# Both heads' choices in one copy, and three exponentials instead of four in the first halves

## The chip, the core and the metric

The kernel runs on one core of a Trainium2 chip. The metric is the device time of one launch in microseconds. The core has five engines that run side by side and wait for each other through semaphores: TensorE (PE in the profile; its weight loads, PEld, are shown apart), VectorE (DVE), ScalarE (ACT), GpSimd (POOL) and SyncE (SP). POOL and SP issue nearly all transfers here, POOL those that also convert float32 to bfloat16. Each engine works through its own instructions in the order in which they are written.

## What is computed

An attention with chunk selection, followed by a feed-forward network with a squared ReLU. There are 4 batches, 8 heads, 768 positions and 64 columns per head. Keys stand in 24 chunks of 32; each query keeps the 6 chunks with the highest upper bound.

```python
k_min = np.min(k_chunks, axis=3)
k_max = np.max(k_chunks, axis=3)
ub = np.sum(np.maximum(q[:, :, :, None, :] * k_min[:, :, None, :, :],
                       q[:, :, :, None, :] * k_max[:, :, None, :, :]), axis=-1)
ub = np.where(causal, ub, -1000000000.0)
top_chunks = np.argsort(ub, axis=-1)[..., -top_k:]
scores = scale * np.matmul(q, k.transpose(0, 1, 3, 2))
...
mask = sel & (pos[:, None] >= pos[None, :])
scores = np.where(mask, scores, -1000000000.0)
...
attn = attn / (np.sum(attn, axis=-1, keepdims=True) + 1e-09)
return np.matmul(attn, v).astype(np.float32)
...
h = np.maximum(x @ w_in, 0.0)
return (h * h @ w_out).astype(np.float32)
```

x has 3072 rows (tokens) and 512 columns (8 heads by 64); w_in is 512 x 2048, w_out 2048 x 512.

## The kernel before

**Slots.** A half is 384 queries of one batch (three tiles of 128). The eight halves run in the order of line 29: batches 0 and 1, first half; batches 0 and 1, second half; then batch 2 and batch 3, each first half and second half. Each half has four slots, one for each pair of heads, so slots 0 to 31 (`slots`, line 219). Slots 0 to 3, 4 to 7, 16 to 19 and 24 to 27 are first halves, 16 slots in all. A first-half query sees three key tiles at most, a second-half query six.

**Steps of a slot.** `step_T` transposes k and q on TensorE (`step_P` calls it in later slots). `extrema` takes minimum and maximum of each key chunk on DVE (L228, L232) and lays them out in `kbds` (L233). `relus_T` makes the positive and negative parts of q on ACT (L288). `place` copies k and q to `kqs` (L293). `step_U` makes the upper bounds `ub` on TensorE (L371 to L382), finds the sixth largest with MAX8 on DVE (L389) and writes with a comparison (L391) which chunks are out: in slots 0 to 3 next to q in `qn0`, in slots 4 to 11 in `chosen`. `step_V` transposes these flags on TensorE into a PSUM tile `qt` and copies them on DVE to rows 64 to 95 of `kqs` (L424 and L428 for slots 0 to 3, L434 and L439 for 4 to 11). From slot 12 on a transfer (`step_W`) does this. A score product therefore has 96 rows, 64 of the head and 32 of flags against a coded one-hot of the key's chunk, and the product itself masks the chunks.

**Scores.** `step_E(s, hh, n)` fills bank n of head hh with score products into a PSUM tile `ps` (L452), takes the exponential on ACT into the SBUF tile `e` (L458) and, for n = 1, lets POOL clear the upper triangle of the three diagonal blocks (`affine_select`, L462). `BANKS` says which key tile and which query tiles go to which columns: a first half has two banks per head, one of 512 columns and one of 256 (at columns 256 to 511); a second half has four. `col_of` finds a block's column again.

**Values.** `step_F(s, hh)` multiplies the blocks of `e` with v, which has a column of ones, into `po` (L478); after the second head DVE takes the reciprocal of the sums (L487) and multiplies (L488) into `x`. From slot 4 on a transposing transfer on SP brings x to `xT` (L492); for slots 0 to 3 `x_T` transposes on TensorE (L516) and `x_copy` copies on DVE (L522).

**Feed-forward.** When a half is done, `push` queues 16 up products (`ffn_up`: four matmuls into `ph`, L560, ReLU on ACT, L564, square on DVE, L566) and 12 down pieces (`ffn_down`: four matmuls each into `py`, L576, copy to `ob`, L582 or L584, and out). `f1()` takes one from the queue between the attention's steps. The first half pushes only up products; its down pieces come with the second `push`. The pieces of one output tile use the rows of w_out in order, the first two of them rows 0 to 1023, the other two the rest.

**PSUM.** `psS` has three banks (score tiles `ps`), `psF` two (`ph`), `psY` one (`py`), `psA` two (tag `att`, line 66). From `psA` come, each time the older of the two: `ub`, `qt`, `po` and the tile of `busy`. A new tile may be written when the last reader of the older one is done.

**Fillers.** `busy(n)` issues n matmuls of the identity into a tile nobody reads (L651).

**Order.** The order is written out by hand. Slots 0 to 3 run in the loop of lines 685 to 718: `step_E(s,0,0)`, k transposes and minimum of slot s+2, `step_E(s,0,1)`, `step_E(s,1,0)`, `busy(8)`, `step_U(s+1)`, `place` of k of slot s+1, `step_E(s,1,1)`, from slot 1 on `step_F(s-1, ...)`, `step_V(s+1)`, then q transposes, `relus_T` and the rest of `extrema` of slot s+2. In slot 3, `x_T` and `x_copy` of the first two pairs stand there, with `busy(10)`. Slots 4 to 31 run in the loop of lines 725 to 856; slot 4 starts with `step_E(4,0,0)`, `step_F(3, ...)`, k and q of slot 5, and `x_T` and `x_copy` of the other two pairs, one by one with `busy(8)` between, then `push(0)`.

**Transfers on POOL.** Loads are queued per slot with `at(slot, ...)` and issued by `go`: codes for batch 1, and w_in in two halves of 1024 columns, in slot 0; three v loads of batch 1 in slot 1; k and q of the third half in slot 2; w_out's first half in slot 3; codes and w_out's second half in slot 4. POOL's selections stand in the same queue.

Of the kernel before, what the change touches and what calls it, by code (L numbers as in the profile page):

```python
# [39 lines left out]
def kernel(  # L40
# [171 lines left out]
    def col_of(half, j, i):  # L212
        for n, bank in enumerate(BANKS[half]):
            for (at, jj, i0, m) in bank:
                if jj == j and i0 <= i < i0 + m:
                    return 512 * n + at + 128 * (i - i0)
        raise KeyError
# [199 lines left out]
    def step_V(s):  # L417
# [14 lines left out]
        qt = psA.tile([128, HB], BF16, tag="att", name="qt")  # L432
        for j in range(j0, HT):
            nc.tensor.matmul(  # L434
                qt[0:2 * CR, 128 * j:128 * (j + 1)],
                lhsT=chosen[s % 2][:, j].rearrange("r h c -> r (h c)"),
                rhs=ident, is_transpose=True, start=True, stop=True)
        for h in range(2):
            nc.vector.tensor_copy(  # L439
                kqs[b % 2][D:KR, p, 2 * half + 1, h, c:], qt[CR * h:CR * h + CR, c:])  # L440

    def step_E(s, hh, n):
        b, half, p = slots[s]
        t = st[s]
        if n == 0:
            t["e"][hh] = work.tile([128, 1920], BF16, tag="e", bufs=4, name="e")
# [21 lines left out]
    def step_F(s, hh):  # L468
# [5 lines left out]
        for i in range(HT):  # L474
            iq = HT * half + i
            for j in range(iq + 1):
                c = col_of(half, j, iq)
                nc.tensor.matmul(  # L478
                    po[:, hh, i, :], lhsT=t["e"][hh][:, c:c + 128],
                    rhs=vn[b % 2][:, 2 * p + hh, j, :],  # L480
                    start=(j == 0), stop=(j == iq))
# [128 lines left out]
    for g in range(2):  # L610
        at(0, load_w_in, 1024 * g, 1024 * g + 1024)
    for j in range(HT):
        at(1, load_vt, 1, j)
    for n in "kq":
# [70 lines left out]
    for s in range(NP):  # L685
# [9 lines left out]
        busy(8)  # L695
        step_U(s + 1)
        if not last:
# [8 lines left out]
        if last:  # L706
            x_T(0, 0, F)
        step_V(s + 1)
        if last:
            x_copy(0, 0, 0, 2, nc.vector.tensor_copy)  # L710
            busy(10)
        else:
            step_T(s + 2, F, Y, "q")
# [11 lines left out]
    for s, (b, half, p) in enumerate(slots):  # L725
# [16 lines left out]
        if s == NP:  # L742
            for n in range(hf):
                step_E(s, 0, n)
            step_F(s - 1, 0)
            step_F(s - 1, 1)
            step_P(s + 1)
            relus_T(s + 1)
            x_T(0, 1, F, (0,))
            x_copy(0, 1, 0, 1, nc.vector.tensor_copy)  # L750
            busy(8, *A)
            x_T(0, 1, F, (1,))
            x_copy(0, 1, 1, 2, nc.vector.tensor_copy)
# [143 lines left out]
```

## Time and profile before

| what | us |
|---|---|
| median of three runs | 268.06 (267.74 to 268.2) |
| the profiled execution, its own time | 268.22 |
| its span, first to last instruction | 266.5 |
| TensorE busy, of the span | 255.0 |
| ScalarE busy | 177.6 |
| VectorE busy | 162.4 |
| GpSimd busy | 92.3 |
| granted TensorE clock, mean | 1.000 |

How to read it: the page gives the busy time of each engine, and matmuls overlap in TensorE's pipe, so the duration of one (219 ns for a filler) is longer than the time from one start to the next. In rows of the timeline stand the start, the time covered, the engine, the line, the operation, output and inputs with their shapes, the count, and in brackets how long the engine had been idle and what ended that. The chain of waits follows the last instruction back: at each step to what released it, or to the instruction before it on its engine; a row has start, length and what it was. Groups have count, then busy time and mean duration in ns, then idle time before them. Stages from here on: the opening is slots 0 to 3, to about 25 us, when the first up product starts; then slots 4 to 7, to about 48 us, when the first down piece starts.

### The profile page before, as it was taken

To read this page: it belongs to the slowest core of one execution; us is meant where nothing else is said; L and a number is where in the kernel's file an instruction comes from. 1 tells how busy PE (TensorE), PEld (TensorE's weight loads), DVE (VectorE), ACT (ScalarE), POOL (GpSimd) and SP (SyncE) were. 2 spreads that over 40 slices of the span, in tenths; PEclk is the share of its full clock that TensorE was granted. 3 is DMA by queue.
4 is the path that set the end of the run, shared out by engine and by line. 5 is a ranking of instruction groups with operands and counts; after the bars stand their busy time and mean duration, and the time that the engine had idled before them with its cause. 6 is when DMAs were issued, how large, how long until landed. Compare 5 with 4: busy or idle time off the path is not lost.

```text
span 266.5 us, 6623 instructions
## 1 busy us (share of the span) xinstructions
PE 255.0 (96%) x2432; PEld 157.8 (59%) x2432; DVE 162.4 (61%) x618; ACT 177.6 (67%) x398; POOL 92.3 (35%) x138
## 2 busy tenths in 40 slices
PE   7789899999999999999999999999999999999995
PEld 7567555556666566655665566745565666645543
DVE  6788999666996468546875576555863233424411
ACT  5898879588976688845575777934685788614500
POOL 8996356426821425235611544320120111000000
PEclk9999999999999999999999999999999999999999
DMA  7999999999997799999995999995532220111022
GB/s 139 163 182 210 170 212 193 134 144 142 147 167 117 140 145 184 131 174 152 190 137 123 131 167 121 222 123 124 127 95 66 71 44 18 57 41 39 2 79 79
DMA packets 116817, 33.98 MB, mean 128 GB/s; under 512 B 103728, under 2 KB 112720, under 8 KB 116784
## 3 DMA queue, kind: packets, MB, share of 16 engines
q0 software_dynamic: 64640, 13.83, 65.5%
q1 hardware_dynamic: 51200, 19.33, 39.6%
q8 instruction: 19, 0.31, 0.5%
q10 hardware_dynamic: 944, 0.39, 0.5%
q14 instruction: 14, 0.11, 0.2%
HBM read 27.26 MB, written 6.29 MB: 126 GB/s over the span
## 4 chain that ended last, share of the span: by engine, by line
PE 79%; DMA 10%; DVE 6%; ACT 3%; issue 1%; SPq 0%; ACTq 0%; DVEq 0%; POOLq 0%
PE py L576 29%; PE ph L560 26%; PE ps L452 12%; DMA w_out<-in_moe_w_out_dram 7%; PE po L478 7%; DMA stage<-in_q_dram 2%; PE ub L375 2%; DVE km L336 2%; PE py L548 1%; ACT e L458 1%; PE idle L651 1%; PE tk L267 1%; DVE x L488 1%; DVE m L389 1%; DVE kq L428 1%
## 5 line engine op out<-in xcount | busy, mean ns | idle before, releaser
L458 ACT ACTIVATE e<-ps 128x512 bf16<-128x512 f32 x192 | 96.3, 551 | 17.6 <-PE ps L452 17.0
L560 PE MATMUL ph<-xT,w_in 128*128 128x384 bf16 x512 | 98.9, 326 | 0.2 <-ACT ht L564 0.2
L576 PE MATMUL py<-w_out,h 128*128 128x512 bf16 x368 | 88.1, 379 | 0.3
L564 ACT ACTIVATE ht<-ph 128x384 bf16<-128x384 f32 x128 | 62.5, 501 | 30.0 <-PE ph L560 29.6
L566 DVE TENSOR_TENSOR h<-ht 128x384 bf16<-128x384 bf16 x128 | 46.6, 374 | 57.4 <-ACT ht L564 56.9
L462 POOL TENSOR_SCALAR_AFFINE_SELECT e<-e 128x384 bf16<-128x384 bf16 x64 | 33.8, 535 | 127.1 <-ACT e L458 126.0
L560 PEld LDWEIGHTS <-w_in 128*128 128x128 bf16 x512 | 47.6, 97 | 30.7 <-issue 1.2
L452 PE MATMUL ps<-kq 96*128 96x384 bf16 (+2 forms) x320 | 57.4, 278 | 2.0 <-DVE kq L428 1.5
L576 PEld LDWEIGHTS <-h 128*128 128x128 bf16 x368 | 34.8, 97 | 35.7 <-issue 1.0
L452 PEld LDWEIGHTS <-kq 96*128 96x128 bf16 x320 | 26.4, 97 | 16.6 <-issue 2.1
L478 PEld LDWEIGHTS <-e 128*128 128x128 bf16 x672 | 25.4, 98 | 4.8 <-issue 0.8
L478 PE MATMUL po<-vn,e 128*128 128x65 bf16 x672 | 26.7, 194 | 0.7 <-DMA vn<-in_v_dram 0.7
L389 DVE MAX8 m<-ub 128x8 f32<-128x16 f32 (+4 forms) x160 | 16.2, 168 | 17.8 <-PE ub L382 10.7
L582 ACT COPY ob<-py 128x512 f32<-128x512 f32 x18 | 10.5, 585 | 24.0 <-PE py L576 23.5
L488 DVE TENSOR_TENSOR x<-po,r 128x384 bf16<-128x384 f32 x32 | 17.8, 558 | 1.1
L109 POOL DMA_DIRECT2D kn<-in_k_dram x15 | 13.3, 896 | 2.2 <-DMA w_out<-in_moe_w_out_dram 1.3
L109 POOL DMA_DIRECT2D qn<-in_q_dram x15 | 13.4, 898 | 0.4 <-DVE km L336 0.2
L336 DVE TENSOR_TENSOR km<-km 128x384 bf16<-128x384 bf16 (+3 forms) x40 | 12.3, 306 | 1.1
L125 POOL DMA_DIRECT2D vn<-in_v_dram x15 | 12.5, 846 | 0.8 <-ACT kq L293 0.4
L375 PEld LDWEIGHTS <-qr 128*128 128x128 bf16 x160 | 7.8, 96 | 4.9 <-DVE qr L316 1.5
L375 PE MATMUL ub<-kbd,qr 128*128 128x48 bf16 (+1 forms) x160 | 9.4, 180 | 1.1 <-DVE kbd L233 0.6
L651 PE MATMUL idle<-ident 128*128 128x128 bf16 x101 | 8.7, 244 | 1.8 <-POOL ident masks.py:199 1.4
(71 smaller groups left out, 178.4 us busy)
## 6 DMA issues: line engine op xcount, KB each, us to landing
out_dram<-ob SPq DMA_DIRECT2D x23, 256.0 KB, 2.5
w_in<-in_moe_w_in_dram POOLq DMA_DIRECT2D x2, 1024.0 KB, 12.1
w_out<-in_moe_w_out_dram POOLq DMA_DIRECT2D x2, 1024.0 KB, 20.4
kn<-in_k_dram POOLq DMA_DIRECT2D x15, 128.0 KB, 5.6
qn<-in_q_dram POOLq DMA_DIRECT2D x15, 128.0 KB, 6.0
kq<-kqT SPq DMA_DIRECT2D x10, 192.0 KB, 4.3
vn<-in_v_dram POOLq DMA_DIRECT2D x4, 384.0 KB, 7.9
vn<-in_v_dram POOLq DMA_DIRECT2D x9, 128.0 KB, 14.9
```

Source lines behind the costliest of these rows:

```text
L109: nc.gpsimd.dma_start(out=nat_of(n, g)[:, DM * j:DM * j + DM].rearrange("p (h d) -> p h d", d=D), in_=rows(n, *ORDER[g], 0, H)[:, 128 * j: ...
L375: nc.tensor.matmul(ub[:, j - j0], lhsT=st[s]["qr"][:, w, 128 * j:128 * (j + 1)], rhs=kbds[b % 2][:, p, w, :, 0:ncs], start=bool(half) and ...
L389: nc.vector.max(out=m8[:, j, hh, :], in_=ub[:, j - j0, hh, 0:12 * half + 4 * j + 4])
L452: nc.tensor.matmul(ps[:, at:at + 128 * m], lhsT=kqs[b % 2][0:KR, p, 2 * (j // HT), hh, 128 * (j % HT):128 * (j % HT + 1)], rhs=qc(s, hh)[: ...
L458: nc.scalar.activation(e[:, 512 * n + lo:512 * n + hi], ps[:, lo:hi], ACT.Exp, scale=float(scale))
L462: nc.gpsimd.affine_select(out=d, in_=d, compare_op=ALU.is_ge, fill=0.0, base=0, channel_multiplier=-1, pattern=[[0, 3], [1, 128]])
L478: nc.tensor.matmul(po[:, hh, i, :], lhsT=t["e"][hh][:, c:c + 128], rhs=vn[b % 2][:, 2 * p + hh, j, :], start=(j == 0), stop=(j == iq))
L488: nc.vector.tensor_mul(x[:, p].rearrange("p j (h d) -> p h j d", h=2), po[:, :, :, 0:D], r.to_broadcast([128, 2, HT, D]))
L560: nc.tensor.matmul(ph[:, 0:HB], lhsT=w_in[:, ki, 128 * f:128 * (f + 1)], rhs=xT[:, ki, :], start=(ki == 0), stop=(ki == NKI - 1))
L564: nc.scalar.activation(ht, ph[:, 0:HB], ACT.Relu)
L566: nc.vector.tensor_mul(h, ht, ht)
L576: nc.tensor.matmul(py[t], lhsT=h2[hb, f][:, 128 * t:128 * (t + 1)], rhs=w_out[:, f, :], start=(f == 0), stop=(f == NFI - 1))
```

## The change

`step_V` of slots 4 to 11 now transposes the flags of each head by themselves, so that both lie on the same 32 rows of `qt`, side by side in columns; one copy takes both to `kqs`. Before, one transpose took both heads' 64 columns to 64 rows, and two copies followed.

In first halves the new `step_E0` takes the place of `step_E`. Both heads share one tile `e` of three banks of 512 columns: head 0's first, head 1's first, and the two second banks of 256 columns together. POOL clears four diagonal blocks after the second bank and two after the third. `step_E(s, 1, 0)` issues nothing there, and `step_E(s, 0, 1)` works on head 1.

The order changes with it: in slots 0 to 3 `step_U` comes ahead of the fillers, which are six instead of eight; in slot 2 q's transposes of slot 4 come ahead of `step_V`; `step_F(3, ...)` moves from slot 4 into slot 3, where `busy(10)` goes; in slot 4 the two pairs' `x_T` and `x_copy` are joined and `busy(8)` goes; w_in's second half is issued in slot 1 behind the three v loads.

```diff
@@ step_V @@
-        qt = psA.tile([128, HB], BF16, tag="att", name="qt")
-        for j in range(j0, HT):
+        qt = psA.tile([128, 2, HB], BF16, tag="att", name="qt")
+        for h in range(2):
+            for j in range(j0, HT):
+                nc.tensor.matmul(
+                    qt[0:CR, h, 128 * j:128 * (j + 1)], lhsT=chosen[s % 2][:, j, h],
+                    rhs=ident, is_transpose=True, start=True, stop=True)
+        nc.vector.tensor_copy(kqs[b % 2][D:KR, p, 2 * half + 1, :, c:], qt[0:CR, :, c:])
+
+    def step_E0(s, n):
+
+        b, half, p = slots[s]
+        t = st[s]
+        if n == 2:
+            return
+        if n == 0:
+            t["e"] = [work.tile([128, 1920], BF16, tag="e", bufs=4, name="e")] * 2
+        e = t["e"][0][:, 512 * min(n, 2):512 * min(n, 2) + 512]
+        ps = psS.tile([128, 512], F32, tag="ps", name="ps")
+        for (hh, at, j, i0, m) in (
+                ((0, 0, 0, 1, 2), (0, 256, 0, 0, 1), (0, 384, 2, 2, 1)),
+                ((1, 128, 0, 0, 3), (1, 0, 2, 2, 1)),
+                (), ((0, 0, 1, 1, 2), (1, 256, 1, 1, 2)))[n]:
             nc.tensor.matmul(
-                qt[0:2 * CR, 128 * j:128 * (j + 1)],
-                lhsT=chosen[s % 2][:, j].rearrange("r h c -> r (h c)"),
-                rhs=ident, is_transpose=True, start=True, stop=True)
-        for h in range(2):
-            nc.vector.tensor_copy(
-                kqs[b % 2][D:KR, p, 2 * half + 1, h, c:], qt[CR * h:CR * h + CR, c:])
+                ps[:, at:at + 128 * m],
+                lhsT=kqs[b % 2][0:KR, p, 0, hh, 128 * j:128 * (j + 1)],
+                rhs=qc(s, hh)[:, 128 * i0:128 * (i0 + m)], start=True, stop=True)
+        nc.scalar.activation(e, ps, ACT.Exp, scale=float(scale))
+        if n:
+
+            d = (t["e"][0][:, 256:768].rearrange("p (a c) -> p a c", c=128) if n == 1 else
+                 e.rearrange("p (h c) -> p h c", h=2)[:, :, 0:128])
+            nc.gpsimd.affine_select(
+                out=d, in_=d, compare_op=ALU.is_ge, fill=0.0, base=0,
+                channel_multiplier=-1, pattern=[[0, d.shape[1]], [1, 128]])
@@ step_E @@
+        if half == 0:
+            step_E0(s, 2 * hh + n)
+            return
@@ transfers @@
-    for g in range(2):
-        at(0, load_w_in, 1024 * g, 1024 * g + 1024)
+    at(0, load_w_in, 0, 1024)
     for j in range(HT):
         at(1, load_vt, 1, j)
+    at(1, load_w_in, 1024, 2048)
@@ slots 0 to 3 @@
         step_E(s, 1, 0)
-        busy(8)
         step_U(s + 1)
+        busy(6)
...
+        if s + 2 == NP:
+            step_T(s + 2, F, Y, "q")
         step_V(s + 1)
         if last:
+            step_F(s, 0)
+            step_F(s, 1)
             x_copy(0, 0, 0, 2, nc.vector.tensor_copy)
-            busy(10)
         else:
-            step_T(s + 2, F, Y, "q")
+            if s + 2 < NP:
+                step_T(s + 2, F, Y, "q")
@@ slot 4 @@
-            step_F(s - 1, 0)
-            step_F(s - 1, 1)
             step_P(s + 1)
             relus_T(s + 1)
-            x_T(0, 1, F, (0,))
-            x_copy(0, 1, 0, 1, nc.vector.tensor_copy)
-            busy(8, *A)
-            x_T(0, 1, F, (1,))
-            x_copy(0, 1, 1, 2, nc.vector.tensor_copy)
+            x_T(0, 1, F)
+            x_copy(0, 1, 0, 2, nc.vector.tensor_copy)
             push(0)
```

`col_of` gets the head as a fourth argument and, for first halves, returns the new columns.

More of the change, by code (lines that the diff above doesn't have):

```diff
@@ L210, with col_of @@
     w_out = consts.tile([128, NFI, DM], BF16, tag="w_out")
-    def col_of(half, j, i):
+    def col_of(half, j, i, hh):
+        if half == 0:
+            return (1024 + 256 * hh + 128 * (i - 1) if j == 1 else
+                    512 + (128 * (i + 1) if j == 0 else 0) if hh else
+                    (256, 0, 128)[i] if j == 0 else 384)
         for n, bank in enumerate(BANKS[half]):
@@ L444, in step_E @@
         t = st[s]
+        if half == 0:
+            step_E0(s, 2 * hh + n)
+            return
         if n == 0:
@@ L476, in step_F @@
             for j in range(iq + 1):
-                c = col_of(half, j, iq)
+                c = col_of(half, j, iq, hh)
                 nc.tensor.matmul(
```

## The prediction

> **What bounds the kernel now.** I read the page first, then the busy time by stage, then the chain of waits, then the timeline where the chain leaves TensorE.
>
> ```profile
> span 266.5 us, 6623 instructions
> PE 255.0 (96%) x2432; PEld 157.8 (59%) x2432; DVE 162.4 (61%) x618; ACT 177.6 (67%) x398; POOL 92.3 (35%) x138
> DMA  7999999999997799999995999995532220111022
> 8.00:25.10 17.10, 14.00 (x236) 11.05 (x237) 14.02 (x51) 15.06 (x38) 15.95 (x24) 1.00 1.41 183
> 25.10:48.30 23.20, 20.49 (x235) 13.07 (x233) 21.47 (x73) 18.42 (x46) 10.80 (x16) 1.00 1.59 189
> 50.30:266.50 216.20, 212.12 (x1873) 127.36 (x1872) 119.84 (x463) 137.44 (x298) 57.56 (x83) 1.00 0.96 116
> ```
>
> The rows by stage give elapsed time, then busy time of PE, PEld, DVE, ACT, POOL, the granted clock, DMA share and GB/s. From 50.3 us on PE is busy 212.12 of 216.20 us: TensorE is the bound there, whatever the others do. From 25.1 to 48.3 us PE stands 2.7 us in all, and DVE, busy 21.47 of 23.20, is as near the limit. In the opening (8 to 25.1 us) nobody is full: a slot is a round trip PE, DVE, PE. The DMA row is 9 from slice 2 on, to past 50 us. What joins the stages is in the chain of waits (start, length, what), and in the timeline at the same place:
>
> ```profile
> 30.53 19.76 DMA w_out<-in_moe_w_out_dram
> 50.33 1.89 PE py L576 x8
> 54.14 0.86 PE py L576 x4
> ...
> 48.34 3.88 PE L576 MATMUL py<-w_out,h 128*128 128x512 bf16 x16
> 50.33 1.39 PEld L576 LDWEIGHTS <-h 128*128 128x128 bf16 x7 [0.39 <-issue]
> ```
>
> The first FFN down products start at 48.34. Eight of them use the first half of w_out; at 0.216 us each (the row of four in 0.86) they are issued by 50.07. The ninth needs the second half, issued at 30.53 and landed at 50.29. So TensorE waits about 0.26 us for a transfer, and **the end is 50.3 plus the TensorE work behind it**. All that is won before 48.34 is swallowed here, unless the transfer lands earlier; a loss before counts only beyond 48.34 + 0.26 = 48.6.
>
> **The change, part by part.**
>
> *Both heads' choices transposed side by side* (slots 4 to 11). Two transposes become four in slots 4 to 7, three become six in 8 to 11; two DVE copies become one.
>
> ```profile
> 14.89 0.54 PE L424 MATMUL qt<-ident,qn 128*96 128x128 bf16 x6 [0.24 <-DVE qn L391]
> 15.36 0.30 PE L260 MATMUL tq<-ident,qn 128*64 128x128 bf16 x4
> 54.93 0.35 PE L434 MATMUL qt<-ident,chosen 128*64 128x128 bf16 x3
> 55.22 0.55 PE L452 MATMUL ps<-kq 96*128 96x128 bf16 x3
> L439 DVE COPY kq<-qt 32x384 bf16<-32x384 bf16 x8 | 2.8, 350 | 1.4 <-PE qt L434 1.2
> L428 DVE COPY kq<-qt 96x768 bf16<-96x768 bf16 x4 | 2.2, 554 | 0.8 <-PE qt L424 0.8
> ```
>
> Six transposes take 0.47 us to the next product (15.36 - 14.89), three 0.29: 0.06 each for the extra ones. Before the pin at 50.3 fall 2 each for slots 5 to 7 and 3 for slot 8, 0.54 us; behind it 3 each for slots 9 to 11: nine, **+0.54 us on the bound engine**. The trace has no transpose of 32 columns of weights; the lower bound is 0.056 (eight plain products of 128 columns in 0.45 us, a row below), the upper 0.097, a third of 0.29. So 0.5 to 0.9; I take 0.54.
>
> The Trainium skill ("TensorE: Matmul & The Clock Gate", Part 4: PE-mode transpose) gives some 275 ns for one transpose inside a kernel. By that figure nine would add 2.5 us and the sum would be 270.6; the rows above, overlapped in the pipe, show less than a quarter of it, and they decide.
>
> On DVE, one copy of 32x768 lies between 350 (32x384) and 554 ns (96x768); I take 554. Two of 350 ran as 0.73 us together (row below), so 0.18 saved per slot, and I take the same for the narrower copies of slots 4 to 7. Where does it count? Once behind the pin:
>
> ```profile
> 74.12 0.73 DVE L439 COPY kq<-qt 32x384 bf16<-32x384 bf16 x2
> 74.14 0.33 DVE kq L439
> 77.33 0.47 PE L375 MATMUL ub<-kbd,qr 128*128 128x48 bf16 x6 [0.22 <-DVE qr L316]
> ```
>
> At 77.33 TensorE stands for DVE, and the chain leads back through slot 11's two copies at 74.14. This wait takes in up to 0.22 of what the last transposes add or the copy saves. So behind the pin: +0.54 less 0.2 = **+0.34**, bounds 0.1 and 0.9.
>
> *One exponential for the second banks.* Each of the 16 first-half slots has three exponentials of 512 columns for two of 512 and two of 256, and seven score products for six, over the same 1536 columns.
>
> ```profile
> L458 ACT ACTIVATE e<-ps 128x512 bf16<-128x512 f32 x38 | 22.1, 600 | 5.4 <-PE ps L452 5.0
> L458 ACT ACTIVATE e<-ps 128x256 bf16<-128x256 f32 x16 | 6.2, 390 | 0.3 <-PE ps L452 0.2
> L462 POOL TENSOR_SCALAR_AFFINE_SELECT e<-e 128x384 bf16<-128x384 bf16 x23 | 12.1, 545 | 18.5 <-ACT e L458 17.5 <-ACT qr L288 1.0
> masks.py:199 POOL TENSOR_SCALAR_AFFINE_SELECT ident<-ident 128x128 bf16<-128x128 bf16 x1 | 0.3, 292 | 0.1
> ```
>
> ACT: 3 x 0.600 against 2 x 0.600 + 2 x 0.390, so -0.18 a slot. It is hidden: behind the pin ACT is busy 137 of 216 us and PE does not wait for exponentials. POOL: two selections of 545 become one of 512 and one of 256 columns; by the slope (253 per 256) 670 + 420, no change. The seventh product only splits 384 columns into 256 + 128:
>
> ```profile
> 124.07 0.22 PE ps L452 x2
> 125.59 0.11 PE ps L452
> ```
>
> Two products of 384 + 128 columns take 0.22 us, one of 256 takes 0.11: the time goes by columns, and one product more costs what the rows' last digit can hide, about 0.01. Eight of these slots lie behind the pin: +0.05 (bounds 0 and 0.2).
>
> *Order on POOL.* w_in's second half goes behind three v loads.
>
> ```profile
> 29.40 0.56 POOL L171 DMA_DIRECT2D kq<-oneh  x1 [4.38 <-DMA w_in<-in_moe_w_in_dram]
> DMA to landing us min/median/max: 19.8/20.4/21.0
> 33.81 0.38 PE L478 MATMUL po<-vn,e 128*128 128x65 bf16 x7 [0.67 <-DMA vn<-in_v_dram]
> 35.92 0.82 PE L560 MATMUL ph<-xT,w_in 128*128 128x384 bf16 x4
> ```
>
> The 0.67 us wait for v goes. w_in's second half, landed by 29.4 now, comes later by the three loads (the last of them ends the wait at 33.81), and the ninth up product that needs it starts at 35.92: 2 us of cover. The codes transfer stood 4.38 us for w_in, the eighth transfer before it; now a v load stands there, and w_out's second half is issued some 3 us sooner than 30.53 (the row of its two landings gives 19.8 to 21.0 us from issue). I take its landing as unmoved: the DMA row shows no empty slice, and the same bytes lie ahead of it. The bounds are -3 (landing follows issue) and +0.3 (the output transposes of slot 6 start sooner and share the engines); I add 0.1.
>
> *Order in the opening.* The ub scores of slot s+1 go ahead of the filler, eight fillers become six; 18 more are dropped in slots 3 and 4, where slot 3's last products move up.
>
> ```profile
> 13.21 0.56 DVE L228 TENSOR_REDUCE km<-tk 128x12 bf16<-128x384 bf16 x1
> 13.59 0.45 PE idle L651 x8
> 14.12 0.54 PE L478 MATMUL po<-vn,e 128*128 128x65 bf16 x12
> 14.19 0.40 DVE L389 MAX8 m<-ub 128x8 f32<-128x8 f32 x4 [0.42 <-PE ub L375]
> 14.63 0.21 DVE L391 TENSOR_TENSOR qn<-ub,m 128x48 bf16<-128x48 f32 x1
> 14.75 0.18 DVE L487 RECIPROCAL r<-po 128x6 f32<-128x6 f32 x1
> 22.22 1.00 POOL L462 TENSOR_SCALAR_AFFINE_SELECT e<-e 128x384 bf16<-128x384 bf16 x2
> 22.36 0.73 PE L651 MATMUL idle<-ident 128*128 128x128 bf16 x10 [0.37 <-DVE x L488]
> PE qt L424 <- DVE qn L391: 1.1, 3, 0.6
> ```
>
> DVE waits 0.42 us for ub, and that goes: MAX8 follows the reduction at 13.77. But ub, filler, po and qt share two PSUM buffers in turn (line 66). Now po gets the filler's, free at once; afterwards it gets ub's, so the 12 products into po at 14.12, hidden under MAX8 today, wait for the comparison L391. That ends 0.42 sooner, at 14.42; 0.54 of products bring the reciprocal to about 14.97 against 14.75: **+0.2 a slot** in slots 1 to 3. Behind these products on PE stand the transposes of V(s+1), and behind the multiply on DVE their copy, for which the next slot's first scores wait. Bounds: -0.42 if the wait is not there, +0.54 if MAX8 gains nothing.
>
> At the end of the opening slot 3's 12 products, with their reciprocal and multiply, move ahead of slot 4's first scores, in place of ten fillers (0.73 us, begun after a wait of 0.37). They read what POOL's selections leave, and POOL ends slot 3's at 23.22, behind the same loads in sum as afterwards, so they cannot go much before 23; the q transposes of slot 4 and the joined x copy only fill. I take 0.2 as won (bounds 0 and 0.7). The first up products start about 0.4 late (-2.0 to +1.6).
>
> Then to 48.34: -0.67 for v, -0.18 x 4 on the full DVE, +0.54 on PE, together -0.85. Arrival 48.34 + 0.4 - 0.85 = 47.9, ahead of 48.6, so TensorE waits at the pin and these terms come to **0**.
>
> Sum against the profiled execution, whose time is 268.22 (the span of 266.5 and 1.7 around it): 268.22 + 0.34 + 0.05 + 0.1 = 268.7. It stands 0.16 above the median of the runs, 268.06, so for a median I forecast 268.5.
>
> **The rivals.** *The landing moves.* For it: issue 3 us sooner, and w_out's halves both took 20 to 21 us from issue. Against: a full DMA row with the same bytes ahead. Then the 0.26 us wait goes too and the arrival counts: -0.26 - 0.45 + 0.4, or, if the opening wins 1.3 (1.7 from my figure), 1.7 less: 266.1 to 267.8, say 267.0.
>
> *The products into po decide, slower.* Place: slots 1 to 3, behind L391. Price: up to 0.54 a slot, 1.6 in all, 1.0 over my figure, and the chain to the first up product takes it whole. It decides once the first down product comes after 48.6: 47.9 + 1.0 = 48.9 is 0.3 past that, and if the DVE saving of 0.7 isn't passed on it is 1.0 past. 268.5 + 0.3 to 1.0: say 269.2. For it: the DVE chain already sets the slot. Against: ACT and DVE are both relieved.
>
> *The clock.* 26 fillers fewer around slots 0 to 4 could lower the granted clock; it is 1.00 in every stage above. At half the clock PE's 14.00 busy us of the opening would take 10.9 more than its 17.10; if that held for a third of the stage, 3.6, the arrival is 51.5, 2.9 past 48.6: 271.4. Against: the longest wait of PE for DVE there is 0.6 us (the last row above: total, times, longest). The Trainium skill ("TensorE: Matmul & The Clock Gate", Why this matters for your kernels) warns of gaps over about 3 us; none here is near it, so by that rule the clock holds.
>
> **How the numbers follow.** My forecast 0.55, its own range 268.0 to 269.0; the landing 0.22; po 0.2; the clock 0.03. A measurement tells about 0.2%, 0.54 us, from no change: slower begins at 268.6, faster below 267.52. The forecast gives 0.01 faster, 0.33 same, 0.21 slower; the landing 0.20 and 0.02 same; the others 0.23 slower. So faster 0.21, same 0.35, slower 0.44. With 0.1 left out at each end, from the landing's far part and from the clock and po's worst, the range is 267.0 to 269.6.
>
> **What would show it.** Right: w_out's second half lands within 0.3 us of 50.3 though issued near 27; TensorE's wait before the ninth down product grows from 0.26 to about 0.7; the v wait and the 4.38 us on POOL are gone; in slots 1 to 3 the products into po begin after L391; six transposes take some 0.4 us, one copy 0.55; behind the pin PE's busy time grows by about 0.5. Wrong: a landing well before 50, a first down product after 48.6, or a clock under 1.00.

## The result and the profile after

The changed kernel takes 268.91 us in the median of 19 runs, the kernel before in as many runs beside it 268.02: a ratio of 1.0034, interval 1.0019 to 1.0049. That is 0.9 us slower. Forecast were 268.5 us and a range of 267.0 to 269.6, with slower the likeliest of the three. The sign is right and the time lies in the range; the account behind them is wrong in several places, as the traces show, so part of the agreement is luck.

The page of the changed kernel, whose profiled execution took 268.84 us with a clock of 1.0:

```profile
span 267.1 us, 6593 instructions
PE 255.0 (95%) x2442; PEld 158.0 (59%) x2442; DVE 161.3 (60%) x609; ACT 176.4 (66%) x382; POOL 92.0 (34%) x138
PE py L609 29%; PE ph L593 25%; PE ps L485 9%; PE po L511 6%; DMA qn<-in_q_dram 3%; DMA kn<-in_k_dram 3%; DVE h L599 2%; PE ps L459 2%; DMA kq<-nsel 2%; PE py L581 1%; DVE km L341 1%; DVE m L394 1%; PE ub L380 1%; ACT ht L597 1%; DVE kq L298 1%
```

Busy times are as before. What is new stands in the chain's row by line: w_out is gone from the chain of this execution, and a transfer kq<-nsel is in it. The busy time by stage (elapsed, PE, PEld, DVE, ACT, POOL, clock, DMA share, GB/s):

```profile
25.45:48.91 23.46, 20.75 (x246) 13.04 (x247) 20.97 (x69) 18.68 (x43) 10.75 (x16) 1.00 1.49 194
48.91:83.90 34.99, 34.91 (x374) 21.54 (x370) 26.16 (x94) 28.42 (x63) 15.69 (x22) 1.00 1.73 145
```

TensorE stands 2.7 us between the first up product and the first down product, as before, and hardly at all from there to 83.9. Then it stands. The timeline of the changed kernel at both places, and the chain of waits at the second:

```profile
48.91 3.61 PE L609 MATMUL py<-w_out,h 128*128 128x512 bf16 x16
84.49 0.60 PE L485 MATMUL ps<-kq 96*128 96x384 bf16 x4 [0.43 <-DMA kq<-nsel]
```

```profile
79.93 4.42 DMA kq<-nsel
84.35 0.14 issue
84.49 0.60 PE ps L485 x4
```

All sixteen down products run through without a gap, in 3.61 us (the timeline before had 3.88 for the same sixteen). The tile view of w_out in the changed kernel says why: the first half was issued at 23.4, the second at 26.7, and 26.75 + 22.5 = 49.2 is earlier than the ninth product needs.

```profile
L638 POOL DMA_DIRECT2D w_out<-in_moe_w_out_dram x2: 898/904/910, 23.4 to 26.7; - x2
DMA to landing us min/median/max: 18.5/20.5/22.5
```

The wait that decides now is another one: slot 12 is the first whose flags come by a transposing transfer on SP (`step_W`). It is issued at 79.93, lands 4.42 us later, and the first score products of slot 12 wait for it. The forecast never looked at this place. In the profile before, the same products start at 83.45, just behind the landing at 83.31, and the timeline names no wait there (from start to start it is 0.27 us, as the table below has it):

```profile
82.22 1.12 PE L478 MATMUL po<-vn,e 128*128 128x65 bf16 x30
83.45 0.60 PE L452 MATMUL ps<-kq 96*128 96x384 bf16 x4
```

### The profile page after: what moved, and what is told of

It is laid out like the page before. It is cut to its first block, busy times and chain, and to the rows that moved or that the text cites. A ratio compares the mean times of both kernels' runs of the same rounds, so it can differ in the third digit from the quotient of the medians.

```text
span 267.1 us, 6593 instructions
## 1 busy us (share of the span) xinstructions
PE 255.0 (95%) x2442; PEld 158.0 (59%) x2442; DVE 161.3 (60%) x609; ACT 176.4 (66%) x382; POOL 92.0 (34%) x138
## 4 chain that ended last, share of the span: by engine, by line
PE 74%; DVE 9%; DMA 7%; ACT 4%; POOL 2%; issue 2%; DVEq 0%; POOLq 0%; ACTq 0%
PE py L609 29%; PE ph L593 25%; PE ps L485 9%; PE po L511 6%; DMA qn<-in_q_dram 3%; DMA kn<-in_k_dram 3%; DVE h L599 2%; PE ps L459 2%; DMA kq<-nsel 2%; PE py L581 1%; DVE km L341 1%; DVE m L394 1%; PE ub L380 1%; ACT ht L597 1%; DVE kq L298 1%
## 5 line engine op out<-in xcount | busy, mean ns | idle before, releaser
L599 DVE TENSOR_TENSOR h<-ht 128x384 bf16<-128x384 bf16 x128 | 47.8, 381 | 57.7 <-ACT ht L597 57.3
L491 ACT ACTIVATE e<-ps 128x512 bf16<-128x512 f32 (+1 forms) x128 | 66.4, 580 | 15.1 <-PE ps L485 14.5
L495 POOL TENSOR_SCALAR_AFFINE_SELECT e<-e 128x384 bf16<-128x384 bf16 x32 | 17.1, 533 | 85.9 <-ACT e L491 81.6
L485 PE MATMUL ps<-kq 96*128 96x384 bf16 (+2 forms) x224 | 37.5, 280 | 1.0 <-DVE kq L443 0.6
L463 ACT ACTIVATE e<-ps 128x512 bf16<-128x512 f32 x48 | 28.3, 597 | 7.5 <-PE ps L459 7.3
L468 POOL TENSOR_SCALAR_AFFINE_SELECT e<-e 128x512 bf16<-128x512 bf16 (+1 forms) x32 | 16.6, 534 | 47.1 <-ACT e L463 47.1
L511 PE MATMUL po<-vn,e 128*128 128x65 bf16 x672 | 26.7, 194 | 0.7 <-DVE kq L443 0.6
L615 ACT COPY ob<-py 128x512 f32<-128x512 f32 x18 | 10.5, 586 | 23.8 <-PE py L609 23.4
L485 PEld LDWEIGHTS <-kq 96*128 96x128 bf16 x224 | 17.8, 97 | 10.8 <-issue 1.2
L459 PE MATMUL ps<-kq 96*128 96x256 bf16 (+2 forms) x112 | 18.3, 257 | 2.1 <-DVE kq L433 1.4
L459 PEld LDWEIGHTS <-kq 96*128 96x128 bf16 x112 | 9.8, 97 | 7.5 <-issue 2.2
```

The source lines that it names most:

```text
L459: nc.tensor.matmul(ps[:, at:at + 128 * m], lhsT=kqs[b % 2][0:KR, p, 0, hh, 128 * j:128 * (j + 1)], rhs=qc(s, hh)[:, 128 * i0:128 * (i0 + m ...
L463: nc.scalar.activation(e, ps, ACT.Exp, scale=float(scale))
L485: nc.tensor.matmul(ps[:, at:at + 128 * m], lhsT=kqs[b % 2][0:KR, p, 2 * (j // HT), hh, 128 * (j % HT):128 * (j % HT + 1)], rhs=qc(s, hh)[: ...
L491: nc.scalar.activation(e[:, 512 * n + lo:512 * n + hi], ps[:, lo:hi], ACT.Exp, scale=float(scale))
L511: nc.tensor.matmul(po[:, hh, i, :], lhsT=t["e"][hh][:, c:c + 128], rhs=vn[b % 2][:, 2 * p + hh, j, :], start=(j == 0), stop=(j == iq))
L599: nc.vector.tensor_mul(h, ht, ht)
```

## The experiments

For each trace I read the same marks: the first score product of slot 0, V (the transposes of the flags) of slots 4 and 5, the first down product, the first score product of slot 12, the end of the span. The wait at slot 12 is taken from start to start, less 0.03 for the usual spacing; the brackets of the timeline give 0.16 less, since they count from the modelled end. Two kernels are not in the table, o_only and e_early_hold: the clock fell in their profiled executions (means of 0.994). The last stretch, behind slot 12's first scores, is called the tail below, and the names with hold are explained there too.

| kernel | first scores to V(4) | V(4) to V(5) | V(5) to first down | to slot 12's scores, without wait | wait | from there to the end | ratio of times (interval) |
|---|---|---|---|---|---|---|---|
| before | 13.36 | 7.37 | 19.27 | 34.84 | 0.27 | 183.03 | 1 |
| after | 13.31 | 7.57 | 19.13 | 34.99 | 0.59 | 182.64 | 1.0034 (1.0019 to 1.0049) |
| v_only | 13.17 | 7.37 | 18.76 | 34.49 | 1.60 | 183.02 | 1.0042 (1.0019 to 1.0065) |
| e_only | 13.01 | 7.32 | 18.90 | 34.39 | 1.72 | 182.65 | 1.0008 (0.9991 to 1.0025) |
| w_only | 13.16 | 7.70 | 18.58 | 34.52 | 0.92 | 183.03 | 1.0014 (0.9997 to 1.0030) |
| a_noV | 12.99 | 8.02 | 18.91 | 34.62 | 1.16 | 182.64 | 1.0018 (0.9990 to 1.0046) |
| b_hold | 13.16 | 7.37 | 18.58 | 34.57 | 0.00 | 183.04 | 0.9975 (0.9951 to 0.9999) |
| a_hold | 13.31 | 7.56 | 19.12 | 34.74 | 0.02 | 182.65 | 1.0009 (0.9978 to 1.0040) |
| v_hold | 13.16 | 7.39 | 18.75 | 34.64 | 0.04 | 183.02 | 0.9997 (0.9972 to 1.0022) |
| e_hold | 12.89 | 7.35 | 18.92 | 34.40 | 0.93 | 182.65 | 0.9993 (0.9968 to 1.0018) |
| ow_hold | 13.14 | 7.57 | 18.57 | 34.89 | 0.00 | 183.03 | 0.9983 (0.9962 to 1.0005) |
| best | 13.16 | 7.37 | 18.58 | 34.53 | 0.00 | 182.66 | 0.9959 (0.9939 to 0.9978) |

For the first two kernels the table adds up to less than the medians suggest. From the first scores to the end the kernel before takes 258.14 us in its profiled execution and the changed one 258.23. Most of the 0.65 us between the two spans lies ahead of the first scores (8.34 and 8.90), where the two programs are the same: that start differs from one execution to the next, and in the kernels of the table it takes 8.34 to 9.23 us. One trace shows where a kernel waits; what a wait is worth in the median, the runs have to say.

**One part alone.** Four kernels hold one part of the change each: the transposes side by side with their joined copy (v_only), the joined exponential (e_only), w_in's second half behind the v loads (w_only), the order of slots 0 to 4 (o_only).

```diff
 v_only, in step_V
-qt[0:2 * CR, 128 * j:128 * (j + 1)], lhsT=chosen[s % 2][:, j].rearrange("r h c -> r (h c)")
+qt[0:CR, h, 128 * j:128 * (j + 1)], lhsT=chosen[s % 2][:, j, h]
 e_only, in step_E
+if half == 0:
+    step_E0(s, 2 * hh + n)
+    return
 w_only
-for g in range(2): at(0, load_w_in, 1024 * g, 1024 * g + 1024)
+at(0, load_w_in, 0, 1024)
 ...
+at(1, load_w_in, 1024, 2048)
 o_only, in the loop of slots 0 to 3 (and step_F, x_T of slots 3 and 4)
-busy(8)
 step_U(s + 1)
+busy(6)
```

> The kernel before with the joined transposes and copy alone. Loop theory (slots 4 to 7 are a round trip in which V's transposes lie, so that what lengthens them reaches the first down piece): first down piece 0.3 to 0.5 us later than before, nine more transposes behind it, in all +0.4 to +0.7 us. Pin theory, as predicted: the first down piece moves, but w_out's second half lands at 50.3 all the same, and only the +0.34 behind it shows.

> The kernel before with the joined exponential alone. Loop theory: the last exponential of slots 4 to 7 has 512 columns instead of 256 and stands on ACT ahead of the q parts of slot s+2, so each slot grows by 0.1 to 0.2 us, the first down piece comes 0.3 to 0.6 us later, in all +0.2 to +0.5. Pin theory: nothing over 0.05 us.

> The kernel before with w_in's second half issued behind the three v loads, and nothing else. Loop theory: the wait of 0.67 for v goes, w_out's second half is issued near 27, the first down piece comes 0 to 0.3 us sooner; total 0 to -0.3. Collision theory: POOL's selections of slot 4, no longer held up by the 4.38 us wait, fall on DVE's squares, MAX8 of slot 5 comes some 0.4 us later and the first down piece 0.2 to 0.4 later. Pin theory: landing at 50.3, total 0.

> The kernel before with the order of slots 0 to 4 alone (ub ahead of six fillers, slot 3's products moved up, joined x copy, fillers of slots 3 and 4 dropped). By the prediction the products into po wait for the comparison in slots 1 to 3 and each slot grows by 0.2 us, the first up product starts 0.4 us late. If po does not wait, as the trace of the changed kernel suggests, slots 1 and 2 take 3.4 us instead of 3.59 and the first up product starts 0 to 0.4 us sooner. Total within 0.3 us of before in both cases.

Medians: 269.12, 268.4, 268.49 and 268.06 us. e_only has the 0.3 us ahead of the first down product that its loop theory gave (18.90 for 18.58 in b_hold), though not because of ACT, as is shown below; the interval of its ratio holds 1. In w_only the collision theory is seen: V(4) to V(5) takes 0.33 us more, the two squares there 0.94 us for 0.61, w_out's second half lands at 49.41, and here too the interval holds 1.

o_only's ratio is 0.9995 (0.9977 to 1.0014). Its clock fell only at 35.9 us. Ahead of that the first up product comes 17.04 us after the first scores, 0.26 later than before and not 0 to 0.4 sooner, as was expected if the products into po do not wait. With the same order ow_hold has 16.37, so the one trace settles little.

Only v_only is clearly slower, by 1.06 us, which is more than either theory had. Yet its trace does not put the loss on TensorE or DVE: with 34.49 us from the first down product it is at slot 12 earlier than the kernel before, and stands there 1.60 us. Timeline and chain of v_only:

```profile
84.49 0.60 PE L450 MATMUL ps<-kq 96*128 96x384 bf16 x4 [1.43 <-DMA kq<-nsel]
```

```profile
79.00 5.36 DMA kq<-nsel
```

The transfer is issued 0.43 us earlier than before (79.00 against 79.43) and lands 1.05 us later (84.36 against 83.31). So its landing does not simply follow its issue; whether it follows what is queued ahead of it, the next runs ask. And behind slot 12's scores only two lengths occur in the table: 183.02 to 183.04 with the old exponentials, 182.64 to 182.66 with the new ones. So the end is set at slot 12, by the landing or by TensorE's arrival, whichever is later; the rest is a constant.

**The traffic ahead of the flags.** The nearest transfer ahead on SP's queue is an output store of 256 KB. I moved it behind the flags and the k transposes that follow them, in the changed kernel (a_hold), in v_only (v_hold) and in the kernel before (b_hold).

```diff
-nc.sync.dma_start(out[r0:r0 + 128, :], ob)
+held.append((r0, ob))
+if not holding[0]:
+    flush()
 ...
+holding[0] = s + 1 == ON_PE * NP
 ...
 for fn, *a in by_sp.get(s, ()):
     fn(*a)
+if s + 1 == ON_PE * NP:
+    holding[0] = False
+    flush()
```

> The changed kernel, with one output store (256 KB, data ready near 78 us) issued behind slot 12's flags and the three k transposes that follow, instead of ahead of them. Theory A (the second wait: slot 12's flags land behind the traffic that is queued ahead of them, and TensorE's work before 84 us is partly hidden there): the flags land at 83.0 or sooner instead of 84.35, TensorE's wait of 0.59 us for them goes, span 266.5, time 268.3, ratio to the kernel before about 1.001. Theory B (the flags' landing does not depend on the store, the loads of q ahead of it set it): landing and wait unchanged, 268.9, ratio 1.0034. Theory C (the time comes from TensorE's own later arrival, the wait is only a replacement): the landing moves but the time stays within 0.2 us of 268.9.

> The kernel before with the transposes side by side and the joined copy only, and the same store held back. Without the store held this version takes 269.1, and its TensorE waits 1.60 us for slot 12's flags. Theory A: the wait goes or shrinks below 0.4, the time falls by 1.2 to 1.6 to about 267.7, ratio 0.998 to 1.000. Theory B: 269.1, ratio 1.004, wait 1.6. Theory D (the nine transposes behind the first pin cost their time on TensorE): the time stays at or above 268.6 even with the wait gone.

> The kernel before with the same store held back. Theory A: its wait of 0.27 us goes, 267.8, ratio 0.999; if its other executions wait as long as the single parts did, up to 1 us less. Theory B: 268.0, ratio 1.000.

The timeline of a_hold, SP's queue and TensorE:

```profile
79.25 1.94 SPq L418 DMA_TRANSPOSE kq<-nsel  x1
82.59 3.84 SPq L325 DMA_TRANSPOSE kqT<-kn  x3
86.52 0.53 SPq L608 DMA_DIRECT2D out_dram<-ob  x1
...
82.25 1.12 PE L511 MATMUL po<-vn,e 128*128 128x65 bf16 x30
83.23 0.60 PE L485 MATMUL ps<-kq 96*128 96x384 bf16 x4
```

Slot 12's scores follow the products into po with no idle time named: the wait of 0.59 is gone, in v_hold that of 1.60 (0.04 is left). Medians are 268.11, 268.45 and 267.60 us. This is theory A for the wait. For the times, a_hold came out as expected (1.0009), b_hold better than its 0.27 us promised: its ratio of 0.9975 is some 0.6 us. That would fit if the kernel before waits longer here in most executions than in its profiled one; no second trace of it shows that. v_hold at 268.45 stayed 0.75 above theory A's 267.7, although its profiled execution, the fastest of its runs, took 267.32. That is close to theory D's 268.6. The marks of that one trace give v_hold 0.28 us more than b_hold (257.00 against 256.72 from the first scores to the end), the medians 0.85. The spread of its runs (267.32 to 269.99) leaves open how often it still waits, and with it what the joined transposes cost in the median.

**Without the joined transposes.**

> The changed kernel with the transposes and copies as before (two or three transposes of both heads' 64 columns, two copies of 32 rows). If the joined transposes are what costs (as the single part at 1.0042 says): 268.0 to 268.3, ratio about 1.000, and by the tail of 182.64 us behind slot 12's first scores instead of 183.03 up to 0.4 less than before. If the cost is a matter of when the traffic ahead of slot 12's flags lands, whatever the part: 268.4 to 268.9, flags landed near 84.2, with a wait of 0.5 or more.

268.78 us, with the flags landed at 84.11 and a wait of 1.16: the trace speaks for the second reading, while the interval of the ratio (0.9990 to 1.0046) does not exclude the first. Taking the transposes out saves TensorE work, and the transfer takes the saving back. V(4) to V(5) is longer here as well, 8.02 for 7.57, since two squares beside POOL's work take 1.52 us; the wait at slot 12 covers that.

**The parts, with the store held.** e_hold has the joined exponential, ow_hold the order and the loads; e_early_hold is e_hold with the joined bank's products and exponential one step earlier, ahead of V.

```diff
 e_early_hold, in step_E0
-if n == 2:
+if n == 3:
     return
 ...
-        (), ((0, 0, 1, 1, 2), (1, 256, 1, 1, 2)))[n]:
+        ((0, 0, 1, 1, 2), (1, 256, 1, 1, 2)), ())[n]:
```

> The kernel before with the store held back behind slot 12's flags, and with the change's exponentials for first halves alone. Theory A (two effects: behind slot 12's first scores each of eight first-half slots is 0.05 us shorter, 0.39 in all; before, in slots 4 to 8, the score products that now stand between V and the q transposes are 512 columns for 256, 0.1 us a slot on a loop that TensorE's own order closes): the stretch from V(5) to the first down product 18.9 us against 18.6 with the old exponentials, the tail behind slot 12's first scores 182.65 against 183.04, span about 0.1 under that of the old exponentials with the store held back (265.95), time 267.5, ratio 0.997. Theory B (the old reading: the joined exponential changes nothing but +0.01 a slot): tail 183.1, V(5) to the first down product 18.6, time 267.7.

> As the one before it, but the joined second-bank products and their exponential go ahead of V, where TensorE stands for the comparison, and not behind it. Theory A: nothing is left between V and the q transposes, the loop of slots 4 to 7 is 0.2 us a slot shorter than with the old exponentials, V(5) to the first down product 17.8 to 18.4 us, tail 182.65 or less, time 266.6 to 267.2, ratio 0.994 to 0.996. Rival (ACT's 0.60 us or the loop through DVE closes the slot, and the place on TensorE does not count): 18.9 as with the late one, 267.5.

> The kernel before with the store held back, and with the change's order of slots 0 to 4 and of the loads alone. Theory A (the order costs about 0.3 before the first down product: first scores to V(4) 13.3 us against 13.16, V(4) to V(5) 7.6 against 7.37): first scores to the first down product 39.4 us against 39.1, tail 183.04, time 267.9, ratio 0.999. Rival (the order is worth what it saves in the opening, about 0.3): 38.8, time 267.3, ratio 0.9965.

*e_hold*: 267.9. The two lengths came as theory A had them (18.92, 182.65), the time did not: 0.4 above. In its trace the flags, issued at 78.61, landed only at 83.25 and TensorE waited 0.93. One store less in front does not always suffice.

Where the 0.3 us between V(5) and the first down product comes from is read from slot 5, in the timelines of b_hold (old exponentials) and of e_only:

```profile
34.85 0.30 PE L434 MATMUL qt<-ident,chosen 128*64 128x128 bf16 x2
35.08 0.28 PE L452 MATMUL ps<-kq 96*128 96x256 bf16 x1
35.30 0.37 PE L267 MATMUL tk<-ident,kn 96*64 96x96 bf16 x8
35.49 0.36 PE L267 MATMUL tq<-ident,qn 96*64 96x96 bf16 x8
...
35.89 0.66 ACT L288 ACTIVATE qr<-tq 128x256 bf16<-128x256 bf16 x2
```

```profile
34.44 0.30 PE L439 MATMUL qt<-ident,chosen 128*64 128x128 bf16 x2
34.67 0.39 PE L461 MATMUL ps<-kq 96*128 96x256 bf16 x2
34.99 0.37 PE L272 MATMUL tk<-ident,kn 96*64 96x96 bf16 x8
35.19 0.36 PE L272 MATMUL tq<-ident,qn 96*64 96x96 bf16 x8
...
35.59 0.66 ACT L293 ACTIVATE qr<-tq 128x256 bf16<-128x256 bf16 x2
```

From V to the ReLU it takes 35.89 - 34.85 = 1.04 us, and 1.15 with the joined bank: between V and the q transposes stand score products of 512 columns (0.32 from start to start) in place of 256 (0.22). The ReLU begins as soon as the q transposes end, and the round trip of the next slot hangs on it. Four transposes for two add as much again: in the changed kernel V starts at 35.10, the products behind it at 35.43, so 0.33 against 0.23. The table adds up: V(5) to the first down product takes 18.58 us in b_hold, 0.18 more with the joined transposes, 0.33 more with the joined exponential, 0.55 more with both.

The 0.39 us won behind slot 12 is at two places. The timelines of b_hold and e_hold at the second of them:

```profile
188.58 0.27 PE L452 MATMUL ps<-kq 96*128 96x256 bf16 x1
188.95 0.47 PE L375 MATMUL ub<-kbd,qr 128*128 128x48 bf16 x6
```

```profile
188.97 0.38 PE L461 MATMUL ps<-kq 96*128 96x384 bf16 x2
189.19 0.42 PE L380 MATMUL ub<-kbd,qr 128*128 128x48 bf16 x6
```

The products into ub of slots 20 and 28 wait for DVE's ReLUs (the expectations name slots 19 and 27, one too few). Before, TensorE had one product of 256 columns to do meanwhile, 0.11 us, and stood 0.26 longer; now it does two, which were done at a place without a wait before, and goes on after 0.22 instead of 0.37. That is 0.15 + 0.11 here. At the first place, near 131 us, the stretch from the scores to the ub products stays 0.43 against 0.42, with 0.11 more work in it. Together 0.36 of the 0.39.

*e_early_hold*: 269.22, ratio 1.0045 (1.0009 to 1.0080), against theory A and above its rival. The tail is 183.02: with the products moved ahead again, nothing fills those waits. The loop did not shorten either: V(5) to the first down product, at 49.76, takes 20.08 us for 18.58, nearly all of it ahead of the fall of the clock at 49.7. And something else appears in the windows of e_early_hold:

```profile
46.00:48.00 2.00, 1.00 (x15) 0.52 (x12) 1.90 (x11) 0.98 (x2) 0.69 (x2) 1.00 2.40 151
48.00:50.00 2.00, 1.47 (x25) 1.15 (x26) 1.09 (x5) 0.62 (x2) 0.54 (x1) 0.91 3.71 114
50.00:52.00 2.00, 2.00 (x6) 0.73 (x5) 1.93 (x6) 1.99 (x5) 1.40 (x3) 0.50 3.13 138
52.00:54.00 2.00, 2.00 (x9) 0.74 (x8) 0.94 (x2) 0.06 (x1) 0.85 (x1) 0.73 2.19 146
```

TensorE is busy 1.00 and 1.47 us in two windows of 2 us, and then the granted clock is 0.50 and 0.73. Five of its twelve executions had a mean clock of 0.981 or 0.994 and took 270.95 to 272.55 us; the seven others, at 0.998 to 1.000, took 267.82 to 269.73.

*ow_hold*: 267.34. First scores to first down product take 39.28 us against 39.11 in b_hold, as theory A had it to 0.1; the time is 0.6 below its figure and at the rival's, and not told apart from b_hold (0.9983 and 0.9975). So neither theory holds whole, and the order of slots 0 to 4 and of the loads is worth nothing here that the times show. V(4) to V(5) is 0.20 longer, which is read from DVE and POOL in the timelines of b_hold and of the changed kernel:

```profile
28.42 0.61 DVE L566 TENSOR_TENSOR h<-ht 128x384 bf16<-128x384 bf16 x2
...
29.45 0.56 POOL L171 DMA_DIRECT2D kq<-oneh  x1 [3.82 <-DMA w_in<-in_moe_w_in_dram]
```

```profile
27.98 1.08 DVE L599 TENSOR_TENSOR h<-ht 128x384 bf16<-128x384 bf16 x2
...
28.22 0.63 POOL L468 TENSOR_SCALAR_AFFINE_SELECT e<-e 128x512 bf16<-128x512 bf16 x1 [0.57 <-ACT e L463]
```

With the old loads POOL stands still for w_in while DVE squares, 0.61 us for two. Now that wait is gone, POOL's selection runs beside the squares, and they take 1.08 us (1.07 in ow_hold). The Trainium skill ("SBUF — State Buffer", Who interferes with whom) says that a DVE instruction with two inputs in SBUF and a GpSimd instruction that reads SBUF hold each other up, one waiting for the whole of the other; the 0.47 us more here, beside a selection of 0.63, agree. So does the rest of the changed kernel's trace: a square that begins under a selection, with at least 0.15 us of it to come, ends 0.20 to 0.23 us after that selection. Most of them take 0.44 us for 0.36, since less than half of the selection is left when they begin.

**The parts that pay.** From the table: the store held back, and the joined exponential only in the first halves behind the second wait, slots 16 to 19 and 24 to 27.

```diff
 e_hold, in step_E and col_of
-if half == 0:
+if half == 0 and s >= ON_PE * NP:
```

> The kernel before with the store held back behind slot 12's flags, and the change's exponentials in slots 16 to 19 and 24 to 27 alone, behind the second wait. Theory A (the joined exponential costs 0.3 us in the loop of slots 4 to 8 and wins 0.39 in the tail, where its later score products fill two waits of TensorE for the ReLUs of slots 19 and 27): V(5) to the first down product 18.6 us as with the old exponentials, tail 182.65, span less the start of the first scores about 256.3 against 256.7 with the store alone, time 267.2, ratio about 0.996. Rival (the 0.39 is an effect of the earlier slots too): tail 183.04, 267.6, ratio 0.9975.

267.19 us, ratio 0.9959 (0.9939 to 0.9978); V(5) to the first down product 18.58, the tail 182.66, no wait at slot 12, span less the start of the first scores 265.53 - 9.23 = 256.30. Each number is theory A's. It is the only version faster than the kernel before by more than 0.2% with its whole interval, and what it has of the change is the joined exponential in eight slots; the store held back is no part of the change.

## Why the prediction was right, and where it was not

The forecast of 0.45 us over the median (0.89 measured) came from three terms, and the runs give each another value. The cleanest comparison is a_hold against b_hold, where the second wait is out of the way. From the table: to V(4) +0.15, to V(5) +0.19, to the first down product +0.54, from there to slot 12 +0.17, behind it -0.39. Sum +0.66; the medians give 268.11 - 267.60 = +0.51. The rest of the 0.89 fits the wait at slot 12, 0.59 against 0.27 in the profiled executions. That the time came out in the range is luck in part: the runs give the terms other sizes and one the other sign, and they partly cancel.

**"The end is 50.3 plus the TensorE work behind it", and all that is won before 48.34 is swallowed.** This is the step that failed. The wait for w_out's second half comes in some executions and not in others. b_hold is the same program as before up to 77 us, and the tile view of w_out there reads:

```profile
DMA to landing us min/median/max: 18.1/18.6/19.1
```

The second half, issued at 30.5, landed at 48.6 and not at 50.29, and no product waited. Apart from the profiled execution of before, only ow_hold waits there at all (0.2 us, landed 50.24); in the other ten kernels of the table the landing is between 48.4 and 49.7. So the 0.54 us of transposes before 48.34, which the forecast set to 0, do count, and a gate exists 34 us later that the forecast did not have: the landing of slot 12's flags.

**The v wait of 0.67 goes, and DVE's saving counts before 48.34.** The wait is gone in the changed kernel, but it was chance as well: V(5) to the first down product is 19.27 in the profile before and 18.58 in b_hold, whose program is the same there. And the loop there is not DVE's alone: TensorE's own order from V over the score products to the q transposes is part of it. With the copy's saving in, that stretch is still 0.17 longer in v_hold than in b_hold (18.75 against 18.58).

**Joined transposes, +0.34 behind the pin.** The sizes of the parts were right, the cover was larger than forecast. Six transposes take 0.44 us to the next product (55.23 to 55.67 in the timeline below), three 0.29, and one copy of 32x768 took 0.55:

```profile
55.23 0.51 PE L440 MATMUL qt<-ident,chosen 128*32 128x128 bf16 x6
55.67 0.56 PE L485 MATMUL ps<-kq 96*128 96x128 bf16 x3
```

From V(8) to V(11) v_hold takes 0.5 us longer than b_hold, for the nine transposes of slots 8 to 10. From V(11) to slot 12's scores it takes 0.25 less, where 0.2 was forecast for the shorter copy. With slot 11's three inside that stretch and slot 8's ahead of the first down product, +0.07 is left behind the first down product for 0.34, and +0.17 before it for 0. These are sizes of single traces; v_hold's median is 0.85 above b_hold's, and where the rest lies is open.

**Joined exponential, +0.05.** Measured are -0.39 behind slot 12 and +0.33 in slots 5 to 8. ACT was indeed no matter. Missed was that the change moves score products: the two second banks of 256 columns stood at two places of the slot, now 512 stand at the later one. The forecast counted columns, which stay the same, and not where TensorE issues them.

**The opening: products into po wait for the comparison, +0.2 a slot.** Wrong. Timeline of the changed kernel, slot 1:

```profile
13.69 0.49 PE L684 MATMUL idle<-ident 128*128 128x128 bf16 x6
14.25 0.54 PE L511 MATMUL po<-vn,e 128*128 128x65 bf16 x12
...
13.93 0.39 DVE L394 MAX8 m<-ub 128x8 f32<-128x8 f32 x4
14.35 0.21 DVE L396 TENSOR_TENSOR qn<-ub,m 128x48 bf16<-128x48 f32 x1
14.82 0.20 DVE L520 RECIPROCAL r<-po 128x6 f32<-128x6 f32 x1 [0.26 <-PE po L511]
```

The products into po begin at 14.25, ahead of the comparison that was to release them. So the two buffers of psA are not handed out strictly in turn, as the description of the kernel has it, and with that step the rival that was built on it falls. MAX8 follows the reduction with no idle time, as forecast. Counted from the first scores (at 8.90 here and 8.34 before), the reciprocals of slots 1 to 3 start at 5.92, 9.33 and 13.09 us, for 6.41, 10.00 and 13.19 before: sooner, and by slot 3 hardly so. Instead of 0.4 late, the first up product comes 16.55 us after the first scores, against 16.78 before and 16.58 in b_hold: nothing.

**Order on POOL.** Timeline of POOL in the changed kernel:

```profile
25.54 0.56 POOL L171 DMA_DIRECT2D kq<-oneh  x1 [0.48 <-DMA vn<-in_v_dram]
26.75 0.90 POOL L638 DMA_DIRECT2D w_out<-in_moe_w_out_dram  x1 [0.66 <-DMA vn<-in_v_dram]
```

The 4.38 us are gone and w_out's second half is issued near 27, as forecast. That its landing would stay within 0.3 of 50.3 is not borne out; at 49.20 it lies in the span of the kernels that issued it at 30.3 (48.4 to 49.7), so the earlier issue did not pull it forward either. The price of the moved loads was another: the squares beside POOL's selections.

**The clock.** In the changed kernel it held in the profiled execution, so the rival did not decide; of the 19 runs two had a lower mean clock (0.994 at 268.93 us and 0.981 at 271.09). But the argument against it, no gap near 3 us, is weaker than it looked. Windows of o_only's profiled execution, and its timeline in the first two:

```profile
32.00:34.00 2.00, 0.88 (x6) 0.36 (x6) 1.66 (x8) 1.70 (x5) 1.56 (x3) 1.00 1.98 174
34.00:36.00 2.00, 0.87 (x15) 0.64 (x16) 0.76 (x3) 0.00 (x0) 0.94 (x2) 0.99 1.58 169
36.00:38.00 2.00, 2.00 (x14) 0.86 (x14) 1.21 (x4) 1.18 (x3) 0.00 (x0) 0.50 1.29 205
```

```profile
33.93 0.33 PE L478 MATMUL po<-vn,e 128*128 128x65 bf16 x5 [0.91 <-POOL e L462]
35.40 0.38 PE L478 MATMUL po<-vn,e 128*128 128x65 bf16 x7 [1.13 <-DMA vn<-in_v_dram]
```

Two gaps of 0.91 and 1.13 us, 1.75 us busy in 4, and the next 2 us run at 0.50. The share of busy time alone does not decide either: in e_only TensorE was busy 2.38 us from 81 to 85, at its wait for the flags, and the clock stayed at 1.00.

**What stays open.** Why the flags of slot 12 land 3.9 us after their issue in one kernel and 5.4 in another, with the same bytes to move, was not settled: in v_only and e_only the k loads on POOL are issued a microsecond later than before, behind k transposes that landed later, but what delayed those was not tried. So the 1.0042 of v_only is traced to the landing in one execution, and no further; that v_hold, with the store moved, is still 0.85 us above b_hold in the median is not explained.

## What to carry to other kernels

A wait of a few tenths on a transfer, in one profiled execution, is not a pin: look for it in a second trace of the same program before setting everything ahead of it to zero. Look too for the next place where the bound engine meets a transfer, even where it comes just in time. When instructions are joined, the count of columns stays but their place moves: read what TensorE does at the old place and at the new one, a wait there is filled or a loop gets longer. And a wait removed on one engine sets its work free to run beside another engine's; ask whose.

## What was not expected of the hardware

The same transposing transfer of flags from SBUF to SBUF lands 2.76 us after its issue in slot 13 of the changed kernel (86.94 to 89.69) and 4.42 in slot 12, behind a store of 256 KB; with the store moved, 3.85 in a_hold, 4.64 in e_hold and 2.89 in the last version. Two DVE squares take 0.61 us alone and 1.08 beside one selection on POOL. And the clock fell to 0.50 after some 4 us in which TensorE was busy 44% (o_only) or 62% (e_early_hold), with no single gap over 1.2 us, while e_only kept it at 60%; the Trainium skill ("TensorE: Matmul & The Clock Gate", Why this matters for your kernels) speaks of idle gaps over about 3 us, which these two traces do not need.
